# Batch 0 sorted in halves, with a Sinkhorn of its own, ahead of a fused attention and dense kernel

## The chip, the cores and the metric

One core of a Trainium2 chip, one launch. The metric is the device time of that launch in microseconds, the median of several runs. A profile of one further execution goes with it; its span runs from the first to the last instruction and is about one microsecond shorter than the time.

The engines: TensorE (PE, with its weight loads shown apart as PEld), VectorE (DVE), ScalarE (ACT), GpSimd (POOL) and SyncE (SP). Each runs its own list of instructions in order. DMA transfers are issued from SP's and POOL's lists and run on 16 shared DMA engines.

## The reference

Sinkhorn-sorted block attention on 4 batches of 8 heads, 768 tokens, 64 wide, followed by a dense layer pair:

```python
P = sort_net                                   # (4, 8, 8, 8), 8 blocks of 96 tokens
for _ in range(5):
    P = np.exp(P - P.max(-1, keepdims=True))
    P = P / (P.sum(-1, keepdims=True) + 1e-9)
    P = P / (P.sum(-2, keepdims=True) + 1e-9)
k_sorted = einsum('bhij,bhjcd->bhicd', P, k_blocks)      # v the same
attn = softmax(scale * q_block @ k_sorted_block.T)       # each block attends to its sorted block
x = (attn @ v_sorted_block) as (3072, 512)
h = x @ w_in                                   # 512 -> 2048
out = (s * relu(h)**2 + b) @ w_out             # 2048 -> 512
```

## The kernel before, in words

The 3072 tokens are eight tiles of 384 (TG): each batch gives two, `half` 0 (blocks 0 to 3) and `half` 1. `ffn1(t)` is the first dense layer of tile t: 8 steps `i`, each 8 matmuls of 128x384 (L361), a relu on ScalarE (L371) and a square on VectorE (L372). `ffn2(t)` is the second: 3 output tiles of 16 matmuls of 128x512 (L382), each ended by a sum with the bias on VectorE (L403) and a store. The order of all work is written out by hand: `manual_schedule` keeps each engine's list as the program issues it, and dictionaries of slots say which pieces of attention are put between the matmuls of the dense layers.

For a batch, `qk_piece` transposes q through a permuted identity and sorts k by the matrix `PD[b]`, 96 matmuls each, evicted in three pieces; `v_piece` sorts v (`permute` first puts v in the order that its matmuls want); `s_piece` forms scores for two heads of a half and takes exp on ScalarE; `p_piece` multiplies by v and divides by the row sums on VectorE (L303, L304); `t_piece` transposes the result on TensorE for batch 0, `t_dma` by DMA for the others.

The steady part runs from batch 1 on: `ffn1` of both tiles of batch b, then `ffn2` of both, in which the attention of batch b+1 is done (`halves`). Ahead of it stands the front:

- SP issues the load of `sort_net` and of v of batch 0 in four pieces (`v0f`); POOL issues q and k of batch 0 in three pieces each, builds the identity, and later w_in in eight pieces, w_out in four, and the next batches.
- The Sinkhorn of all four batches runs at once in 32 partitions: six or seven small VectorE operations (L184 to L194) and one exp (L177) for each of five steps. ScalarE copies one quarter of v between the steps (L156). TensorE warms up on zeros (L149).
- `build_pd(b)` spreads batch b's matrix to 128 partitions with a float matmul (L201) and five VectorE operations. Batch 0's stands in the front, the other three in `ffn1(1)`, where the bias is also summed (`make_bias`, L466 to L474).
- Then q, v and k of batch 0 are sorted whole, all of half 0's attention and the first two score pieces of half 1 follow, and `ffn1(0)` begins with three steps held open (`ahead=3`). The rest of half 1's attention stands in the slots of `ffn1(0)`.

PSUM is two pools: `psa` with three buffers of two banks, `psb` with two of one.

Of the kernel before, what the change touches and what calls it, by code (L numbers as in the profile page):

```python
# [22 lines left out]
def kernel(  # L23
# [47 lines left out]


    sn = const.tile([BH, NB, NB], FP)
    nc.sync.dma_start(out=sn, in_=sort_net.rearrange("b h i j -> (b h) i j"))
    v0f = gtp.tile([128, C2, D], FP, tag="gt", name="v0f")
    CV = C2 // 4
    for c in range(0, C2, CV):
        nc.sync.dma_start(out=v0f[:, c:c + CV, :].rearrange("p c d -> p (c d)"),  # L78
                          in_=raw[2][0][:, c * D:(c + CV) * D])

    RAW = {}

    def load(t, b, parts=1):
        ti = rawp.tile([128, C2, D], BF, tag=f"raw{t}", name=f"raw{t}")
        RAW[t, b] = ti
        n = C2 // parts
        for c in range(0, C2, n):
            nc.gpsimd.dma_start(out=ti[:, c:c + n, :].rearrange("p c d -> p (c d)"),
                                in_=raw["qkv".index(t)][b][:, c * D:(c + n) * D])

# [17 lines left out]
    nc.vector.memset(KS[0][:, :, :, C2:GAP], 0.0)  # L108
    eps = const.tile([BH, NB], FP)
    nc.vector.memset(eps, 1e-9)  # L110

    load("q", 0, 3)
    load("k", 0, 3)


    ident = const.tile([128, 128], BF)
    make_identity(nc, ident)
    idv = ident.rearrange("p (a e j z) -> p a e j z", a=NHP, e=2, j=NB)
    qid = const.tile([128, 2, 2, NHP, NB], BF)
    for e in range(2):  # L120
        nc.gpsimd.tensor_copy(out=qid[:, e], in_=idv[:, :, e].rearrange("p a j z -> p z a j"))
    emat = const.tile([BH, B, 128], FP)
    nc.gpsimd.memset(emat, 0.0)
    nc.gpsimd.affine_select(out=emat, in_=emat, pattern=[[-H, B], [-1, H], [0, 2 * NB]], base=0,
                            channel_multiplier=1, compare_op=ALU.not_equal, fill=1.0)
    wi = const.tile([128, NHP, d_ff], BF)
    wo = const.tile([128, NF, d_model], BF)

    def load_w():
        wiv = moe_w_in.rearrange("(a p) f -> p a f", p=128)  # L130
        for c in range(2):
            cs = slice(c * (d_ff // 2), (c + 1) * (d_ff // 2))
            for a in range(NHP):
                nc.gpsimd.dma_start(out=wi[:, a, cs], in_=wiv[:, a, cs])
        fill_vs(0)
        wov = moe_w_out.rearrange("(f p) n -> p f n", p=128)
        for c in range(4):
            fs = slice(c * (NF // 4), (c + 1) * (NF // 4))
            nc.gpsimd.dma_start(out=wo[:, fs, :], in_=wov[:, fs, :])
# [6 lines left out]
    def warm(n):  # L146
        for _ in range(n):
            z = psb.tile([128, 512], FP, tag="b", name="z")
            nc.tensor.matmul(out=z, lhsT=zeros[:, 0:128], rhs=zeros, start=True, stop=True)  # L149


    def permute(eng, b, src, cs=slice(0, C2), ds=slice(0, D)):
# [4 lines left out]
        else:  # L157
            eng.tensor_copy(out=o, in_=i)  # L158


    rstat = const.tile([BH, NB], FP)
    rrec = const.tile([BH, NB], FP)
    jsel = const.tile([128, NB], FP)
    bm = const.tile([128, 2 * 2 * NHP], FP)
    idle = [
        lambda: nc.vector.tensor_reduce(
            out=jsel, in_=ident.rearrange("p (h j z) -> p j h z", h=H, j=NB), axis=AX.XY, op=ALU.add),
        lambda: nc.vector.tensor_reduce(
            out=bm.rearrange("p (e z a) -> p e z a", e=2, z=2),
            in_=idv.rearrange("p a e j z -> p e z a j"), axis=AX.X, op=ALU.add),  # L170
    ]
    nc.vector.tensor_reduce(out=rstat, in_=sn, axis=AX.X, op=ALU.max)
    nc.vector.tensor_tensor(out=sn, in0=sn, in1=rstat.broadcast_to([BH, NB, NB]),
                            op=ALU.subtract)
    warm(30)
    for it in range(5):
        nc.scalar.activation(out=sn, in_=sn, func=AF.Exp)  # L177
        if it >= 1:
            permute(nc.scalar, 0, v0f, slice((it - 1) * CV, it * CV))
        if it == 2:  # L180
            load_w()
        if it in (1, 2):
            idle[it - 1]()
# [3 lines left out]
        if it == 4:  # L187
            break
# [8 lines left out]
    PD = {}  # L197

    def build_pd(b):
        pe = psb.tile([128, 512], FP, tag="b", name="pe")  # L200
        nc.tensor.matmul(out=pe[:, 0:NB * NB], lhsT=emat[:, b, :],  # L201
                         rhs=sn.rearrange("p i j -> p (i j)"), start=True, stop=True)
        tmp = rtp.tile([128, NB, NB], FP, tag="tmp", name="tmp")
        nc.vector.tensor_tensor(out=tmp, in0=pe[:, 0:NB * NB].rearrange("p (i j) -> p i j", j=NB),
# [10 lines left out]
            in0=spread(bm, [list(bm.ap[1]), [0, NB]]), scalar=rc,  # L215
# [3 lines left out]
    def evac(eng, out, in_):  # L219
        if eng == "A":  # L220
            nc.scalar.copy(out=out, in_=in_)  # L221
        else:
            nc.vector.tensor_copy(out=out, in_=in_)  # L223

    QT = {}

    def qk_piece(t, b, c0, eng, first=None):
        if t == "q" and c0 == 0:
            QT[b] = trp.tile([128, NG, 2, C2], BF, tag="qt", name="qt")
        src = RAW[t, b]  # L230
        mov = qid.rearrange("p e z a j -> p e z (a j)") if t == "q" else PD[b]
        dst = QT[b] if t == "q" else KS[b % 2]
        ps = psa.tile([128, CK, 2, NG], FP, tag="a", name="tp")
        for c in range(CK):
            for e in range(2):
                nc.tensor.matmul(out=ps[e * 64:(e + 1) * 64, c].rearrange("p z g -> p (z g)"),  # L236
                                 lhsT=src[:, c0 + c, :],
                                 rhs=mov[:, e].rearrange("p z g -> p (z g)"),
                                 start=True, stop=True)
        if first is not None:  # L240
            first()
        evac(eng, dst[:, :, :, c0:c0 + CK], ps.rearrange("p c z g -> p g z c"))
# [14 lines left out]
    def s_piece(b, half, hp):  # L257
        g0 = hp * NB + half * HB
        sc = psa.tile([128, 2, 512], FP, tag="a", name="sc")
        for n in range(HB):  # L260
            for e in range(2):
                pr = slice(e * 64, (e + 1) * 64)
                nc.tensor.matmul(out=sc[:, e, n * BLK:(n + 1) * BLK],  # L263
                                 lhsT=KS[b % 2][pr, g0 + n].rearrange("p z c -> p (z c)"),
                                 rhs=q_of(b, pr, hp, half * HB + n),
                                 start=True, stop=True)
        at = atp.tile([KR, 2, TG], BF, tag="at", name="at")
        nc.scalar.activation(out=at, in_=sc[0:KR, :, 0:TG], func=AF.Exp, scale=scale)  # L268
        AT[b, half, hp] = at

    def s_banks(b, half, hp):

        g0 = hp * NB + half * HB
        sc = [psb.tile([128, TG], FP, tag="b", name="scb") for _ in range(2)]
        for n in range(HB):
            for e in range(2):
                pr = slice(e * 64, (e + 1) * 64)
                nc.tensor.matmul(out=sc[e][:, n * BLK:(n + 1) * BLK],
                                 lhsT=KS[b % 2][pr, g0 + n].rearrange("p z c -> p (z c)"),
                                 rhs=q_of(b, pr, hp, half * HB + n),  # L280
                                 start=True, stop=True)
        at = atp.tile([KR, 2, TG], BF, tag="at", name="at")
        for e in range(2):
            nc.scalar.activation(out=at[:, e], in_=sc[e][0:KR], func=AF.Exp, scale=scale)
        AT[b, half, hp] = at
# [62 lines left out]
    def ffn1(t, slots, ahead=0):  # L348
# [16 lines left out]
        for i in range(ahead):  # L365
            part(i, (0, 1))
# [184 lines left out]
```

## Time and profile before

| | |
|---|---|
| median of 3 runs | 237.34 us (235.2 to 239.28) |
| the profiled execution, span | 236.1 us |
| TensorE, VectorE, ScalarE, GpSimd busy | 221.3, 122.9, 98.2, 55.4 us |
| first matmul of sorted v | 14.59 us |
| first dense layer of tile 0 begins | 31.84 us |
| second dense layer of tile 0 begins | 58.99 us |
| first dense layer of tile 2 begins | 91.08 us |
| each further batch | 50.0 us |

The times in the second part are starts in the profiled execution, from the timeline of TensorE's rows. The profile lists, for each engine, busy time and groups of like instructions by line; a waits view that says what ended the idle time before an instruction ("issue" where nothing in the profile did); a chain of the work that ended last; and busy time by stages, with the clock that TensorE was granted as a share of full speed.

### The profile page before, as it was taken

What the parts mean: (1) busy time and instruction counts of PE and PEld (TensorE: products, weight loads), DVE (VectorE), ACT (ScalarE), POOL (GpSimd) and SP (SyncE); (2) the same over time, 40 slices, a digit from 0 to 9 for tenths busy, and PEclk for the clock granted to TensorE, in tenths of its full rate; (3) what the DMA queues carried; (4) which work ended last, traced back from release to release, by engine and by line L of the source; (5) the groups of instructions that cost most, each with busy time, mean ns of one, the idle gap of its engine ahead of it and who ended that gap; (6) DMA issues with size and microseconds to landing.
All of it is one profiled execution on the core that took longest, in us unless ns stands there. A gap on an engine that the chain in (4) does not pass through costs nothing.

```text
span 236.1 us, 5888 instructions
## 1 busy us (share of the span) xinstructions
PE 221.3 (94%) x2584; PEld 130.8 (55%) x2607; DVE 122.9 (52%) x236; ACT 98.2 (42%) x123; POOL 55.4 (23%) x89
## 2 busy tenths in 40 slices
PE   7874898999998999999999999999999999999994
PEld 3553565655564655565555656656455656554453
DVE  6663426669755476444644764446355754342221
ACT  4783538554311524565212335665015255660000
POOL 7547500993663992000000000000000000000000
PEclk9998579999999999999999999999999999999999
DMA  6999999949999934920021187400112352001122
GB/s 144 286 210 193 206 209 218 190 74 205 137 190 203 170 67 124 147 37 0 3 89 50 44 114 160 86 3 3 44 47 88 64 119 45 0 1 47 52 81 90
DMA packets 37674, 25.03 MB, mean 106 GB/s; under 512 B 29200, under 2 KB 31504, under 8 KB 37648
## 3 DMA queue, kind: packets, MB, share of 16 engines
q0 software_dynamic: 17744, 12.85, 36.7%
q1 hardware_dynamic: 19904, 11.81, 20.3%
q8 instruction: 20, 0.33, 0.6%
q14 instruction: 6, 0.05, 0.1%
HBM read 27.27 MB, written 6.29 MB: 142 GB/s over the span
## 4 chain that ended last, share of the span: by engine, by line
PE 84%; DMA 4%; ACT 4%; issue 4%; DVE 2%; SPq 1%; DVEq 0%
PE hps L361 34%; PE ops L382 34%; DMA v0f<-in_v_dram 4%; PE tv L248 4%; PE tp L236 3%; PE pv L298 3%; PE sc L263 3%; PE ops L395 1%; ACT rt L371 1%; DVE x L304 1%; ACT qt L221 1%; PE z L149 1%; ACT vp L156 1%; PE tr L318 1%; SPq L78 1%
## 5 line engine op out<-in xcount | busy, mean ns | idle before, releaser
L361 PE MATMUL hps<-xt,wi 128*128 128x384 bf16 x512 | 86.3, 327 | 0.7 <-DVE x L304 0.5
L382 PE MATMUL ops<-wo,gt 128*128 128x512 bf16 x347 | 81.5, 379 | 2.2 <-issue 1.6
L371 ACT ACTIVATE rt<-hps 128x768 bf16<-128x768 f32 x64 | 51.7, 812 | 42.7 <-PE hps L361 41.1
L361 PEld LDWEIGHTS <-wi 128*128 128x128 bf16 x512 | 49.2, 98 | 32.9 <-issue 0.9
L372 DVE TENSOR_TENSOR gt<-rt 128x768 bf16<-128x768 bf16 x64 | 36.5, 572 | 44.4 <-ACT rt L371 44.2
L382 PEld LDWEIGHTS <-gt 128*128 128x128 bf16 x368 | 33.7, 98 | 37.0
L403 DVE SCALAR_TENSOR_TENSOR ot<-ops,s_bc,bias 128x512 f32<-128x512 f32 (+1 forms) x25 | 18.2, 729 | 37.2 <-PE ops L382 33.7
L268 ACT ACTIVATE at<-sc 112x768 bf16<-112x768 f32 x30 | 22.6, 809 | 32.7 <-PE sc L263 32.7
L158 POOL COPY vp<-rawv 128x384 bf16<-128x384 bf16 x24 | 20.3, 907 | 10.6 <-DMA rawv<-in_v_dram 10.6
L304 DVE TENSOR_TENSOR x<-pv,rec 96x512 bf16<-96x512 f32 x32 | 22.0, 687 | 1.1
L298 PEld LDWEIGHTS <-at 112*128 112x128 bf16 (+1 forms) x256 | 13.6, 106 | 7.2 <-ACT at L268 1.0
L223 DVE CAST vs<-tv 112x1024 bf16<-112x1024 f32 x11 | 13.3, 1223 | 6.6 <-PE tv L248 6.6
L99 POOL DMA_DIRECT2D qtok<-in_q_dram x16 | 12.4, 781 | 11.7 <-DMA rawv<-in_v_dram 6.7
L248 PE MATMUL tv<-pd,vp 128*64 128x64 bf16 x512 | 10.4, 197 | 5.0 <-issue 4.0
L221 ACT CAST vs<-tv 112x1024 bf16<-112x1024 f32 x5 | 5.1, 1021 | 22.9 <-PE tv L248 22.9
L298 PE MATMUL pv<-vs,at 112*128 112x66 bf16 (+1 forms) x256 | 14.6, 202 | 0.0
L248 PEld LDWEIGHTS <-vp 128*64 128x64 bf16 x512 | 9.2, 113 | 8.3 <-issue 7.3
L149 PE MATMUL z<-zeros 128*128 128x512 bf16 x37 | 11.9, 463 | 1.9 <-DVE zeros L103 1.2
L303 DVE RECIPROCAL rec<-pv 96x8 f32<-96x8 f32 x32 | 6.4, 200 | 13.9 <-PE pv L298 13.9
L263 PE MATMUL sc<-qt,ks 64*128 64x96 bf16 x240 | 9.0, 218 | 0.4 <-ACT vs L221 0.4
L223 DVE CAST ks<-tp 128x1024 bf16<-128x1024 f32 x7 | 8.3, 1218 | 0.2
L149 PEld LDWEIGHTS <-zeros 128*128 128x128 bf16 x39 | 4.0, 111 | 6.8 <-issue 2.8
(69 smaller groups left out, 107.9 us busy)
## 6 DMA issues: line engine op xcount, KB each, us to landing
out_dram<-ot SPq DMA_DIRECT2D x23, 256.0 KB, 2.0
rawv<-in_v_dram POOLq DMA_DIRECT2D x3, 768.0 KB, 11.9
rawk<-in_k_dram POOLq DMA_DIRECT2D x3, 768.0 KB, 7.9
wi<-in_moe_w_in_dram POOLq DMA_DIRECT2D x8, 256.0 KB, 11.8
wo<-in_moe_w_out_dram POOLq DMA_DIRECT2D x4, 512.0 KB, 14.2
v0f<-in_v_dram SPq DMA_DIRECT2D x4, 384.0 KB, 6.8
qtok<-in_q_dram POOLq DMA_DIRECT2D x16, 96.0 KB, 10.0
rawq<-in_q_dram POOLq DMA_DIRECT2D x3, 256.0 KB, 7.1
```

The source lines that it names most:

```text
L149: nc.tensor.matmul(out=z, lhsT=zeros[:, 0:128], rhs=zeros, start=True, stop=True)
L158: eng.tensor_copy(out=o, in_=i)
L223: nc.vector.tensor_copy(out=out, in_=in_)
L248: nc.tensor.matmul(out=ps[z * GAP:(z + 1) * GAP, d, :], lhsT=VP[b % 2][:, d0 + d, :], rhs=PD[b][:, :, z, :], start=True, stop=True)
L268: nc.scalar.activation(out=at, in_=sc[0:KR, :, 0:TG], func=AF.Exp, scale=scale)
L298: nc.tensor.matmul(out=pv[0:m, e, n * VW:(n + 1) * VW], lhsT=atf[:, c0:c0 + m], rhs=VS[b % 2][:, e * NG + g0 + n, :], start=True, stop=True)
L304: nc.vector.tensor_tensor(out=x[:, :, hp * 128:(hp + 1) * 128].rearrange("p n (e d) -> p e n d", e=2), in0=pvv[:, :, :, 0:D], in1=rec.unsq ...
L361: nc.tensor.matmul(out=H1[i][:, f, 0:TG], lhsT=wi[:, hp, fc:fc + 128], rhs=xt[:, :, hp, :], start=(hp == 0), stop=(hp == NHP - 1))
L371: nc.scalar.activation(out=rt, in_=h, func=AF.Relu)
L372: nc.vector.tensor_tensor(out=gt[:, 2 * i:2 * i + 2, :], in0=rt, in1=rt, op=ALU.mult)
L382: nc.tensor.matmul(out=ops, lhsT=gt[:, f, m * 128:(m + 1) * 128], rhs=wo[:, f, :], start=(f == 0), stop=(f == NF - 1))
L403: nc.vector.scalar_tensor_tensor(out=ot[:, ns], in0=ops, scalar=s_bc, in1=BIAS[0][:, ns], op0=ALU.mult, op1=ALU.add)
```

## The change

Batch 0's Sinkhorn becomes one of its own in 64 and 128 partitions, taking row sums by a float matmul against a mask (`rs`), with five VectorE and ScalarE operations for a step and v's quarters copied half by ScalarE, half by VectorE between the steps. The matrix comes out in two halves of columns (`pd0`). Only half 0 of k and v (blocks 0 to 3) is sorted ahead of `ffn1(0)`, by `kh` and `vh`, each with 32-column operands; half 1 stands in the slots of `ffn1(0)`. q of batches 0 and 1 is loaded in halves in another layout and transposed with the plain identity (`q_piece`, `q_half`). The other batches' Sinkhorn, still for all four together, runs inside `ffn1(1)` and `ffn2(0)` (`sink`), and their `build_pd` in `ffn2(0)` and `ffn2(1)`. w_in is loaded by columns, 512 at a time, and the identity is built ahead of POOL's loads. The first `part`s of `ffn1` are placed one by one in place of `ahead`.

```diff
+    s0 = const.tile([HI, NB], FP)
+    nc.sync.dma_start(out=s0, in_=sort_net[0].rearrange("h i j -> (h i) j"))
...
+    sn = const.tile([BH, NB, NB], FP)
+    nc.sync.dma_start(out=sn, in_=sort_net.rearrange("b h i j -> (b h) i j"))
+
+    ident = const.tile([128, 128], BF)
+    make_identity(nc, ident)
...
+    load_qh(0, 0, slice(0, 4))
     load("k", 0, 3)
+    load_qh(0, 0, slice(4, 8))
+    fill_vs(0)
+    load_wi(0, 512, slice(0, 2))
+    load_wi(0, 512, slice(2, 4))
+    load_wi(512, 1024)
+    load_qh(0, 1, slice(0, 8))
+    load_wi(1024, 1536)
+    load_wi(1536, 2048)
...
+    for it in range(4):
+        nc.scalar.activation(out=ex, in_=src, func=AF.Exp, scale=crec)
+        permute0(it)
...
+        nc.tensor.matmul(out=rs[:, 0, 0:NB], lhsT=msk.rearrange("p h g -> p (h g)"), rhs=ex,
+                         start=True, stop=True)
+        if it == 3:
+            q_piece(0, 0, 0, "A")
+            warm(2)
+        elif it == 2:
+            warm(3)
+        else:
+            warm(50, 16, 64)
+        nc.vector.reciprocal(out=rr, in_=rs[:, 0, 0:NB])
...
+        nc.vector.reciprocal(out=crec, in_=csum)
...
+    pd0(0)
...
+    kh(0, 0, "A", psa)
+    kh(0, 1, "D", psa)
+    pd0(1)
+    kh(0, 2, "A", psa)
+    vh(0, 0, "D", psb)
+    vh(0, 1, "A", psb)
+    vh(0, 2, "D", psa)
     s_piece(0, 0, 0)
+    vh(0, 3, "D", psa)
+    q_piece(0, 0, 2, "A")
     s_piece(0, 0, 1)
...
+    part(0, 0, (0,))
+    t_piece(0, 0, 1, "D")
     s_piece(0, 0, 3)
+    part(0, 0, (1,))
     p_piece(0, 0, 2)
+    kh(1, 0, "A", psb)
     p_piece(0, 0, 3)
+    part(0, 1, (0, 1))
...
+        if n == 1:
+            s0 = {0: [SK(3)], 1: [SK(4)], 2: [PDB(1)],
+                  4: [K(n, 0, "D"), K(n, 1, "A"), K(n, 2, "D")],
+                  7: [QF(n, 0, "D"), QF(n, 1, "A")],
+                  9: [V(n, 0, "D"), V(n, 1, "A"), V(n, 2, "D")]}
...
-    ffn1(0, {0: [SB(2)], 1: [P(0, 1, 0)], 2: [SB(3)], 3: [P(0, 1, 1)], 4: [P(0, 1, 2)],
-             5: [P(0, 1, 3)], 6: [TP(0, 1, 0, "A")], 7: [TP(0, 1, 2, "D")]}, ahead=3)
-    ffn1(1, {1: [PDB(1)], 3: [PDB(2)], 4: [make_bias], 6: [PDB(3)]}, ahead=3)
+    ffn1(0, {0: [KH(1, "D")], 1: [KH(2, "A"), QP(0, "D")],
+             2: [VH(0, "D"), VH(1, "A")], 3: [SC(0, 1, 0), VH(2, "D")],
+             4: [VH(3, "D"), SC(0, 1, 1)], 5: [P(0, 1, 0), QP(2, "D")],
+             6: [SC(0, 1, 2), P(0, 1, 1), TP(0, 1, 0, "A")],
+             7: [SC(0, 1, 3), P(0, 1, 2), TP(0, 1, 1, "D")]}, {0: 2, 1: 2})
+    part(1, 0, (0, 1))
+    p_piece(0, 1, 3)
+    t_piece(0, 1, 2, "A")
+    part(1, 1, (0, 1))
+    t_piece(0, 1, 3, "D")
+    ffn1(1, {2: [make_sel], 3: [SK(0)], 4: [make_bias], 5: [SK(1)], 7: [SK(2)]}, {0: 2, 1: 2})
     s0, s1 = halves(1, [(5, LD("k", 3)), (6, LD("v", 3)), (7, lambda: load_q_rows(3))])
+    s1[1] = [PDB(2)]
+    s1[2] = [PDB(3)]
```

`SK(it)` is `sink(it)`, one step of the loop that stood in the front before: on VectorE a row sum, reciprocal, product, column sum, reciprocal, product, with one exp on ScalarE ahead; step 0 has a maximum and a subtraction ahead of it and an added eps, step 4 ends after the first product.

## The prediction

> **What bounds the kernel now.** The page first: which engine fills the span, and whether its clock held.
>
> ```profile
> PE 221.3 (94%) x2584; PEld 130.8 (55%) x2607; DVE 122.9 (52%) x236; ACT 98.2 (42%) x123; POOL 55.4 (23%) x89
> PEclk9998579999999999999999999999999999999999
> q8 instruction: 20, 0.33, 0.6%
> ```
>
> TensorE fills 94%, so only its idle stretches and its slow stretch can be won. The clock row dips once, in the fourth to sixth slice (18 to 35 us). The third line is TensorE's own instructions: 20 packets for 5204 of them, 256 each. Next the chain in order of time, for the places where TensorE did not set the pace.
>
> ```profile
> 2.61 9.50 DMA v0f<-in_v_dram
> 12.13 1.50 ACT vp L156
> 13.63 1.83 ACT qt L221 x2
> ...
> 18.21 1.04 PE tv L248 x59
> 19.25 3.04 issue
> ...
> 32.05 2.77 PE hps L361 x16
> ...
> 59.42 0.59 PE ops L382 x2
> ...
> 91.24 20.80 PE hps L361 x128
> ```
>
> To 12.13 the chain is the load of v. At 19.25 TensorE stops for 3.04 us and waits for no engine. From 59 on (second dense layer) it is TensorE's rows nearly alone; from 91.24 the periods repeat, and no row of them is edited. So the change is worth what it does to two times: the start of the second dense layer (58.99) and its end (91.08). The stages around the stop, by the columns PE, PEld, DVE, ACT, POOL, clock, DMA share, GB/s:
>
> ```profile
> 18.82:22.23 3.41, 0.43 (x27) 0.35 (x22) 1.16 (x1) 0.44 (x1) 2.18 (x3) 0.96 1.09 183
> 22.23:25.64 3.41, 2.66 (x39) 1.67 (x40) 0.00 (x0) 2.98 (x4) 3.22 (x9) 0.50 1.12 204
> 25.64:29.05 3.41, 3.23 (x38) 2.33 (x40) 2.27 (x6) 0.87 (x3) 1.47 (x3) 0.50 1.23 206
> 29.05:32.47 3.42, 3.08 (x36) 2.27 (x35) 1.50 (x4) 2.24 (x3) 0.54 (x1) 0.54 1.25 207
> ```
>
> After the stop the clock is 0.50 for 10.2 us, and the DMA engines are full. Last the timeline, for the prices on VectorE:
>
> ```profile
> 7.42 0.21 DVE L184 TENSOR_REDUCE rstat<-sn 32x8 f32<-32x64 f32 x1
> ...
> 8.65 0.21 DVE L194 TENSOR_TENSOR sn<-sn,rrec 32x64 f32<-32x64 f32 x1
> 9.03 0.25 ACT L177 ACTIVATE sn<-sn 32x64 f32<-32x64 f32 x1
> ...
> 55.06 0.73 DVE L468 TENSOR_SCALAR bias<-cps,b_bc 32x512 f32<-32x512 f32 x1
> 55.83 2.31 DVE L471 SCALAR_TENSOR_TENSOR bias<-cps,b_bc,bias 32x512 f32<-32x512 f32 x3
> ```
>
> A Sinkhorn step is six VectorE rows from 7.42 to 8.86, 1.44 us, and an exp between, 0.45 with its hops; the bias sum holds VectorE 3.08.
>
> **The front, to the first dense layer.** Batch 0's own Sinkhorn with row sums on TensorE saves nothing by itself: its last step still copies v's last quarter, which lands at 12.12 now and, with the same loads sharing the engines, again. Without that cover the chain could end 1 to 2 us sooner. After 12.12 come the VectorE half of the copy (0.45: the 1024-element cast is 1.22, so 384 are about 0.45), reciprocal, product, reciprocal (0.2 each, 0.05 between) and the first half's matrix (0.28): 13.65. Before, the matrix was done at 14.09 and its first matmul, behind two qt evictions on ScalarE, ran at 14.59. So 0.9 won. The little warming matmuls (16 columns) lie between the row sums; bounds are the 64-column pair, 17 ns, and the 66-column pv, 32 ns, so 0.9 to 1.6 us for fifty, within a step of 1.9. I take them as free; at half clock they would be 3.2 and make the start up to 2 us later.
>
> Now the stop. It came before TensorE's row 698, a second (0.93, at 71.99) before row 1969. With float matmuls counted as the four records each leaves, these are 701 and 1981: 1280 apart, five blocks of 256. So TensorE waits for instructions, and the block edges lie at 189, 445, 701 and so on. Edge 445 was passed at 16.5, the block behind 701 usable at 22.29: 5.8 us later, with the DMA full. In the changed list five float matmuls stand ahead, so the edges are rows 430 (in the third half-k piece) and 686 (start of the fourth half-v piece). A piece is 32 pairs of 17 ns, 0.55. From 13.65, row 430 falls at 14.9 and row 686 is reached at 17.2; the block is there at 14.9 + 5.8 = 20.7. The stop stays, 3.5 us, and 1.6 is won against 22.29. Halved columns may make a pair cheaper than 17 ns (8.5 at the least), which would only lengthen this wait. The Trainium skill ("Runtime: NRT & Kernel Launch", Instruction fetch mechanics) has the same blocks but says the fetch is mostly hidden; by it the wait would fall out, here it measured 3.04.
>
> From 20.7 the half-tile pieces run as a relay. Rest of v 0.55, q transposes 0.4 (12 by the 0.043 of tr at most 0.5), ScalarE's qt copy 0.8 and exp 0.81, pv, then VectorE's reciprocal and product 0.95, transposes and copies 0.5, twice over since scores 2 and 3 come late, and the half-1 k piece 0.55: the rest of the first dense layer starts at 29.2 with eight of its matmuls done (31.84 before, with none).
>
> **Inside the first dense layers.** First tile: 56 matmuls by 0.1625 (20.8 for 128) are 9.1. Put in: two k and four v pieces 3.3, 24 transposes 0.8, four scores 1.0, three pv 0.8, eight tr 0.35. Together 15.4, and about 1.6 of waits for buffers that VectorE empties late: 46.2. The split doubles k's and v's instructions, and this half stands on TensorE's path. Then the tile's end: relu 0.81, square 0.55, reciprocal and product 0.95, copy 0.3 until the next tile's second quarter, and again pv, 0.95, tr, 0.3: 51.3, of which 2.6 is work. Second tile: 9.0 and the bias matmuls 1.0. The second dense layer starts at 61.2, against 58.99: **2.2 lost**, although three pe matmuls have left this stage.
>
> **The new wait.** The other batches' Sinkhorn now stands on VectorE between the squares, and PDB(1), after 12 matmuls of the second layer, waits for its last product. VectorE's rows from 55.4 on, in program order: selectors 0.6; five squares with gaps 2.9; step 0 (max, subtract, exp, seven rows) 2.5; bias 3.1; steps 1 and 2, 1.46 each; step 3 with its exp 1.8; step 4 with its exp 1.1; 0.5 of waits for a relu and an exp. 15.4: done at 70.8. Nothing hides this: but for those waits VectorE is never idle in it, and the first output tile's sum and store stand behind it too. TensorE stands at PDB(1) at 61.2 + 2.6 = 63.8, and behind it are all of the second layer, k, q and v of batch 1. **6.9 lost.** Each PDB is 0.36 on TensorE and moves behind the 58.99 mark: **1.1**. q of batch 1 by 48 transposes instead of 96 matmuls (1.64): between 0.8 at 17 ns and 2.1 at 0.043; I take 1.5, **0.1 won**.
>
> After 6.9 idle the clock will drop, since 3.04 was enough. Coming back cost 10.2 us of half clock in sparse work (5.1 lost) and, at the start, 4.0 in dense warm matmuls (2.0 lost: rows 0.43 apart until 4.98, later 0.21). The second layer is dense, so near the lower: **2.3**. The Trainium skill ("TensorE: Matmul & The Clock Gate", Part 1) gives one window of 3.4 us for the return, 1.7 by it; the 10.2 here is three.
>
> Put at nothing: w_in by columns, q in halves, constants and wo are the same bytes at 205 GB/s; w_in's first columns land near 17 and are used at 24.7, its last near 27 (used 41), wo near 38 (used 56), sn near 13 (used 56.7). The selector pattern now goes ahead of POOL's first load, 0.6; k's last third then lands near 13 and is used at 14.7. Without these covers each would cost its own lateness. q's runs are shorter (384 bytes; qtok's 128-byte loads took 10 us), with ten or more to spare.
>
> **Sum.** 2.2 + 6.9 + 1.1 - 0.1 + 2.3 = 12.4. The profiled execution spans 236.1; the median is 237.34, 1.2 more, which I keep: 236.1 + 12.4 + 1.2 = **249.7 us**.
>
> **Rivals.** (1) The wait at PDB(1) is short: for it, VectorE is only 52% busy over the span, and before it was just 1.4 late at 60.41 though it had three PDBs and the bias in this stage. Without the wait and its clock loss, 249.7 - 6.9 - 2.3 = **240.5**, not slower by 2%. It decides once the wait is below 1.6. Against: 15.4 of rows with no gap. (2) The fetched block comes in time: 249.7 - 3.5 = **246.2**. For it, instruction packets after 30 us started within 2 us of their edge; against, the DMA is as full as it was then. (3) The 3.5 stop drops the clock in the front too, as 3.04 did: the relay's TensorE rows are 5 us, doubled, with some 2 hidden in its waits, plus 3: **252.7**. Against: the stop may straddle two of the clock's windows.
>
> **How the numbers follow.** Forecast 0.47, (3) 0.25, (2) 0.15, (1) 0.10, something that makes it really faster 0.03. (2) without the 2.3 of clock and with the six inner pieces at half price (1.7 less) is 242.2; (3) with the 5.1 return is 255.5. Low 242, high 255.5; the forecast's own range is 247 to 251.5. This measurement tells about 2% from no change: 232.6 and 242.1. Faster 0.03, within 0.10, slower 0.87.
>
> **What would show it.** Right: a wait of TensorE near 7 us just after the second layer starts, released by VectorE's last sn row; VectorE without idle time ahead of it; an issue gap of 3 us at a half-v piece; the clock row dipping near 65 to 75; periods from the third tile on unchanged at 50.0. Wrong: second layer starting before 59, or PDB(1) unwaited.

## The result and the profile after

The changed kernel takes 257.13 us (median of four, 254.47 to 258.12) against 238.06 (four, 235.2 to 239.28): a ratio of 1.083, 95% interval 1.072 to 1.094. It is slower, as forecast, but by more: 249.7 had been predicted and 255.5 was the upper end. The profiled execution is the fastest of the four (254.47, span 252.3), 16.2 us longer than before's span.

The page: the share of TensorE first, its clock, its instruction packets.

```profile
PE 232.4 (92%) x2810; PEld 141.6 (56%) x2832; DVE 128.7 (51%) x273; ACT 97.1 (38%) x131; POOL 57.8 (23%) x86
PEclk9999999999976999999999999999999999999999
q8 instruction: 22, 0.36, 0.6%
```

There is one dip, at 70 to 80 us, and none in the front. That is a trap: the trace has no clock record before 28.6 us, and the row then shows full speed. The rows themselves tell the clock. The chain in order of time:

```profile
6.78 2.77 PE z L129 x50
...
10.07 2.77 PE z L129 x50
...
17.30 2.67 PE kh L309 x48
19.97 2.56 PE vh L323 x48
...
23.14 1.84 issue
...
107.15 20.80 PE hps L490 x128
```

The chain of the front is no longer the load of v. It is the two blocks of fifty small warming matmuls (128x64 by 16 columns), 57 ns each, then the half pieces, then the stop. From 107 us the periods are 50.0 us as before. From TensorE's timeline, the points that the prediction dated (in square brackets the idle time ahead of a row and what ended it):

```profile
17.23 2.74 PE L309 MATMUL kh<-pdh,rawk 128*64 128x32 bf16 x96
...
24.97 0.99 PE L323 MATMUL vh<-pdh,vp 128*64 128x32 bf16 x30 [1.84 <-issue]
...
34.44 0.86 PE L490 MATMUL hps<-xt,wi 128*128 128x384 bf16 x4 [0.24 <-ACT xt L236]
...
67.39 2.54 PE L514 MATMUL ops<-wo,gt 128*128 128x512 bf16 x11
75.50 0.66 PE L353 MATMUL pe<-sn,emat 32*128 32x64 f32 x2 [5.57 <-DVE sn L340]
```

Three half-k pieces take 2.74, 0.91 each; in the first dense layer one takes 0.68. So the front ran at half clock. The second dense layer starts at 67.39 instead of 58.99 (8.4 lost) and its pair ends 39.6 later instead of 32.1 (7.5 lost); together 15.9 of the 16.2. Who waited, and the stretch around the new wait (columns as in the prediction):

```profile
PE pe L353 <- DVE sn L340: 5.6, 1, 5.6
...
DVE rr L286 <- PE rs L277: 4.7, 3, 2.2
```

```profile
65.00:70.00 5.00, 4.87 (x26) 2.35 (x24) 4.72 (x11) 2.40 (x4) 1.47 (x2) 1.00 0.73 49
70.00:75.00 5.00, 0.00 (x0) 0.00 (x0) 3.94 (x18) 0.77 (x3) 1.67 (x2) 0.80 0.00 0
75.00:80.00 5.00, 4.50 (x28) 1.92 (x30) 2.19 (x8) 0.00 (x0) 0.00 (x0) 0.51 0.06 22
```

VectorE is busy 4.7 of 5 us ahead of the wait, TensorE does nothing for 5.6, and then runs at half clock to 79.9. That half of the prediction came as told. The second line of the waits is the one that had not been priced: VectorE stands 4.7 us for row sums, and 4.0 of them behind the two blocks of small matmuls:

```profile
10.11 0.21 DVE L286 RECIPROCAL rr<-rs 128x8 f32<-128x8 f32 x1 [2.21 <-PE rs L277]
...
13.40 0.21 DVE L286 RECIPROCAL rr<-rs 128x8 f32<-128x8 f32 x1 [1.79 <-PE rs L277]
```

### The profile page after: what moved, and what is told of

Same layout as the page of the kernel before. It is cut to its first block, busy times and chain, and to the rows that moved or that the text cites. A ratio compares the mean times of both kernels' runs of the same rounds, so it can differ in the third digit from the quotient of the medians.

```text
span 252.3 us, 6386 instructions
## 1 busy us (share of the span) xinstructions
PE 232.4 (92%) x2810; PEld 141.6 (56%) x2832; DVE 128.7 (51%) x273; ACT 97.1 (38%) x131; POOL 57.8 (23%) x86
## 4 chain that ended last, share of the span: by engine, by line
PE 84%; DVE 8%; ACT 3%; issue 3%; DMA 1%; DVEq 0%; ACTq 0%
PE ops L514 31%; PE hps L490 30%; PE pv L442 3%; PE sc L420 3%; PE z L129 3%; PE tv L398 3%; PE vh L323 2%; PE tp L388 2%; DVE gt L503 2%; PE ops L527 1%; PE kh L309 1%; ACT rt L502 1%; DVE x L448 1%; DVE bias L612 1%; PE rs L277 1%
## 5 line engine op out<-in xcount | busy, mean ns | idle before, releaser
L514 PE MATMUL ops<-wo,gt 128*128 128x512 bf16 x347 | 83.4, 385 | 2.2 <-issue 1.6
L503 DVE TENSOR_TENSOR gt<-rt 128x768 bf16<-128x768 bf16 x64 | 35.9, 561 | 47.4 <-ACT rt L502 47.2
L428 ACT ACTIVATE at<-sc 112x768 bf16<-112x768 f32 x16 | 12.1, 806 | 21.0 <-PE sc L420 21.0
L424 ACT ACTIVATE at<-sc 112x768 bf16<-112x768 f32 x16 | 12.5, 808 | 12.3 <-PE sc L420 12.3
L116 POOL DMA_DIRECT2D qtok<-in_q_dram x16 | 12.3, 778 | 10.2 <-DMA rawv<-in_v_dram 5.2
L238 DVE CAST vs<-tv 112x1024 bf16<-112x1024 f32 x9 | 10.7, 1221 | 5.9 <-PE tv L398 5.9
L129 PE MATMUL z<-zeros 128*64 128x16 bf16 (+1 forms) x127 | 12.4, 238 | 1.4 <-DVE zeros L120 1.2
L129 PEld LDWEIGHTS <-zeros 128*64 128x64 bf16 (+1 forms) x128 | 7.9, 155 | 3.5 <-issue 2.1
L236 ACT CAST vs<-tv 112x1024 bf16<-112x1024 f32 x3 | 3.1, 1018 | 16.8 <-PE tv L398 16.8
L323 PE MATMUL vh<-pdh,vp 128*64 128x32 bf16 x256 | 6.7, 199 | 1.8 <-issue 1.8
L238 DVE CAST ks<-tp 128x1024 bf16<-128x1024 f32 x6 | 7.1, 1220 | 1.8 <-PE tp L388 1.6
```

The costliest lines, as they stand in the source:

```text
L129: nc.tensor.matmul(out=z[0:m, 0:w], lhsT=zeros[:, 0:m], rhs=zeros[:, 0:w], start=True, stop=True)
L424: nc.scalar.activation(out=at.rearrange("p e (t c) -> p e t c", c=CQ), in_=sc[0:KR, :, 0:TG].rearrange("p e (c t) -> p e t c", c=CQ), func ...
L503: nc.vector.tensor_tensor(out=gt[:, 2 * i:2 * i + 2, :], in0=rt, in1=rt, op=ALU.mult)
L514: nc.tensor.matmul(out=ops, lhsT=gt[:, f, m * 128:(m + 1) * 128], rhs=wo[:, f, :], start=(f == 0), stop=(f == NF - 1))
```

## The experiments

Three theories were set against each other. A: the small warming matmuls delay the row sums and leave the clock low. B: VectorE's late Sinkhorn makes TensorE wait at the pe matmul. C: TensorE's front is paced by the fetch of its own instructions. The rival to A was that the halved pieces and the order of loads cost the front.

**Wide warming in place of small.**

```diff
-    warm(16, 16, 64)
+    warm(2)
...
-            warm(50, 16, 64)
+            warm(6)
```

> The changed kernel with its small warming matmuls (64x16) replaced by 512-column ones of the same half-clock time: 16 small by 2 wide, each fifty by 6 wide. Theory A (the front ran at half clock to 29 us because small matmuls do not bring the clock up, and their 57 ns each delay the row sums): half-k pieces fall from 0.91 to 0.55 us each, the second dense layer of tile 0 starts near 61 instead of 67.4, span 245 to 247 against 252.3. 102 fewer TensorE rows also move the instruction-block edge out of the short pieces, so the 1.84 us stop should be gone, which is counted in this. Rival (the halved k and v pieces and the order of the loads cost the front): pieces at full clock perhaps, but the second layer still starts at 65 or later, span 250 or more. The wait at the pe matmul of batch 1 stays near 5.6 under both.

Measured: 254.62 us, 1.071 of before (1.066 to 1.076), span 251.8.

```profile
6.71 2.72 PE L129 MATMUL z<-zeros 128*128 128x512 bf16 x6
9.48 1.46 PE L129 MATMUL z<-zeros 128*128 128x512 bf16 x6
...
14.17 1.69 PE L309 MATMUL kh<-pdh,rawk 128*64 128x32 bf16 x96 [0.43 <-DVE pdh L260]
...
21.10 0.61 PE L323 MATMUL vh<-pdh,vp 128*64 128x32 bf16 x15 [3.97 <-issue]
...
65.34 2.54 PE L514 MATMUL ops<-wo,gt 128*128 128x512 bf16 x11
```

The same six matmuls take 2.72 and then 1.46: the clock came up at 9.5. A half-k piece is 0.56, and the first one starts 3.1 us earlier. So far theory A holds. But TensorE then stands 3.97 us for instructions instead of 1.84, the clock falls (the next half-v piece takes 1.04), and only 2 us are left at the second layer. The expectation that the stop would go was wrong by its own arithmetic: a matmul with its weight load is two instructions, so 102 fewer move the edge by 204 of a block of 256, that is 26 matmuls earlier. The stop came 15 matmuls before the end of half-v piece 2 instead of 2 into piece 3, with 8 score matmuls between: 25. By its numbers (65.34 and 251.8) the rival came true in this run; the run that issues the weights later, below, tells the two apart.

**No small matmuls at all.**

```diff
-    warm(16, 16, 64)
...
-        else:
-            warm(50, 16, 64)
```

> The changed kernel with the small warming matmuls left out and nothing in their place. It tells their two costs apart. Theory A, delay: the four row sums come at VectorE's own pace, first half-k matmul near 14.5 instead of 17.2. Theory A, clock: TensorE is idle between the row sums, so it stays at half clock (a half-k piece still 0.9 us, matmuls of 512 columns 0.43 apart) to about 29 us; second dense layer of tile 0 starts near 63, span about 248. Rival (the small matmuls did hold something up, and the clock falls lower or later without them): second layer later than 67.4, span above 252.

Measured: 254.02, 1.069 (1.064 to 1.075), span 250.8.

```profile
13.76 2.74 PE L306 MATMUL kh<-pdh,rawk 128*64 128x32 bf16 x96
...
20.55 0.19 PE L320 MATMUL vh<-pdh,vp 128*64 128x32 bf16 x1 [1.49 <-issue]
...
32.89 1.22 PE L487 MATMUL hps<-xt,wi 128*128 128x384 bf16 x4 [0.24 <-ACT xt L236]
...
66.00 2.54 PE L511 MATMUL ops<-wo,gt 128*128 128x512 bf16 x11
```

Without them the first half-k matmul comes at 13.76, where the prediction had put it (13.65), against 17.23. That is the whole delay. The second layer, though, starts only 1.4 earlier than in the changed kernel (63 had been expected). Now compare this kernel with the wide warming at the stop: one ran the pieces at half clock, the other at full. By the prediction's count a stop lies one block, 128 matmuls, behind the edge at which the block is asked for. Counted from that edge (15.4 here, 14.9 there), the block came after 5.1 and 6.2 us. Half clock did not lengthen the fetch; it only let TensorE reach the stop later. The clock counts behind the stop, where this kernel, at half clock until 33.8, took 12.3 us to the rest of the first layer, and the other, at half clock until 26.5, took 10.6.

**The pe matmul later.**

```diff
-            s0 = {0: [SK(3)], 1: [SK(4)], 2: [PDB(1)],
-                  4: [K(n, 0, "D"), K(n, 1, "A"), K(n, 2, "D")],
-                  7: [QF(n, 0, "D"), QF(n, 1, "A")],
-                  9: [V(n, 0, "D"), V(n, 1, "A"), V(n, 2, "D")]}
+            s0 = {0: [SK(3)], 1: [SK(4)],
+                  4: [QF(n, 0, "D"), QF(n, 1, "A")], 6: [PDB(1)],
+                  8: [K(n, 0, "D"), K(n, 1, "A"), K(n, 2, "D")],
+                  10: [V(n, 0, "D"), V(n, 1, "A"), V(n, 2, "D")]}
```

> The changed kernel with the pe matmul of batch 1 moved from slot 2 to slot 6 of the second dense layer of tile 0, its q transposes ahead of it in slot 4, k to slot 8 and v to slot 10. The front is unchanged. Theory B (TensorE stands 5.6 us for VectorE's last Sinkhorn row and then runs 6.8 us at half clock): the wait falls to 0 to 1 us, no slow stretch follows, span 252.3 - 5.6 - 2.3 + 0.5 = 245. Rival (VectorE is the bound of this stage, so the wait only moves to the k copies, the output sums or the scores of batch 1): span 249 or more, with a new wait of 3 us or more behind slot 6.

Measured: 249.76, 1.049 (1.042 to 1.057), span 248.0.

```profile
32.44 1.04 PE L309 MATMUL kh<-pdh,rawk 128*64 128x32 bf16 x32
...
69.34 4.26 PE L514 MATMUL ops<-wo,gt 128*128 128x512 bf16 x19
...
77.45 0.40 PE L353 MATMUL pe<-sn,emat 32*128 32x64 f32 x2 [0.55 <-DVE sn L340]
```

The wait is 0.55, no slow stretch follows (pe 0.40), and the pair takes 33.4 instead of 39.6: 6.2 won, B holds. The front is the same code as in the changed kernel, and yet the second layer starts 2 us later: the half-k piece at 32.44 still takes 1.04, the clock came up at about 38 us here and at 29 in the profiled execution of the changed kernel. So one and the same front varies by 2 us between two executions.

**The kernel before with small warming.**

```diff
-    warm(30)
+    warm(5)
+    warm(105, 16, 64)
```

> The kernel before, with its 30 warming matmuls of 512 columns at the start replaced by 5 of them and 105 small ones (64x16), so that TensorE still issues without a gap to about 9 us. Theory A (small matmuls do not bring the clock up): the 64 q matmuls that took 1.20 us take about 2.4, the k and v pieces double too, the clock comes up late, first dense layer starts 2 to 4 us later than 31.8, span 238 to 240. Rival (any matmul without a gap brings it up): 1.20 as before, span 236 to 237.

Measured: 237.15, 0.999 of before (0.995 to 1.003), span 233.3.

```profile
9.04 1.92 PE L238 MATMUL tp<-qid,rawq 128*64 128x64 bf16 x62
...
20.61 0.71 PE L238 MATMUL tp<-pd,rawk 128*64 128x64 bf16 x21 [2.49 <-issue]
...
30.73 2.77 PE L363 MATMUL hps<-xt,wi 128*128 128x384 bf16 x16
```

The same q matmuls in the kernel before:

```profile
9.61 1.20 PE L236 MATMUL tp<-qid,rawq 128*64 128x64 bf16 x64
```

The clock part of A is right: 62 matmuls take 1.92, where 64 took 1.20, though TensorE had issued without a gap since 1.2. (The first clock record is at 17.3 us, behind the wider q and v pieces.) Its price is not: the first dense layer starts at 30.73, 1.1 earlier than in the kernel before. Half clock ahead of the stop is hidden by the wait for instructions. What counts is the stretch behind the stop, and there this kernel was at full clock from 24.2 us where the kernel before was not until 32.2.

**Theory C by itself: weights issued later.** In the changed kernel with wide warming, POOL holds back most of the weights until half-v piece 2 has been copied (`gsc` is one element, s and b go with them):

```diff
     vh(0, 2, "D", psa)
+    nc.gpsimd.tensor_copy(out=gsc, in_=VS[0][0:1, 0, 0:1])
+    for f0 in (512, 1024, 1536):
+        load_wi(f0, f0 + 512)
...
+        nc.gpsimd.dma_start(out=wo[:, fs, :], in_=wov[:, fs, :])
```

> The changed kernel with the wide warming matmuls, and in addition the loads of w_in from column 512 on, of the two scalars and of w_out are issued by POOL only after half-v piece 2 has been copied, so that the DMA engines are nearly idle when TensorE's next block of instructions is fetched. Theory C (the front is bound by the instruction fetch: one block of 128 matmuls each 5 to 6 us while the loads fill the DMA engines; the stop was 3.97 us with wide warming alone): the stop falls to 1.5 us or less, the clock then stays up, second dense layer of tile 0 starts at 61 to 62 against 65.3, span 247 to 248. Rival (the fetch takes its 6 us whatever the load): stop 4 us, 65.3 and 251.8 as without the later loads; or the later weights come too late for the first layer and TensorE waits for wi.

Measured: 255.4, 1.066 (1.059 to 1.074), span 250.6: stop 3.48, second layer at 64.23. A miss for the test more than for the theory: the loads issued ahead kept the DMA share at 1.25 from 14 to 16 us, when the block was asked for. The same with the edit of the late pe matmul:

> Wide warming, later loads and the late pe matmul together: all three suspected costs of the changed kernel taken away at once. If they add: second layer at 61 to 62, no wait at the pe matmul, span 248.0 - 69.3 + 61.5 = 240, a time near 242. What then is left over the kernel before (some 2 to 4 us) is the halved k and v pieces and the pe matmuls inside the dense layers. Rival (VectorE is late whatever the slot once the front is faster, since its Sinkhorn then starts no earlier): wait at pe of 2 to 4 us and a span of 243 to 246.

Measured: 247.5, 1.041 (1.036 to 1.046), span 245.6, where 242 and 240 had been expected: stop 3.23, second layer at 65.79, wait at pe 0.57. The kernel before got the same cure, behind its second k piece:

```diff
-            load_w()
+            fill_vs(0)
...
     qk_piece("k", 0, CK, "D")
+    nc.gpsimd.tensor_copy(out=gsc, in_=KS[0][0:1, 0, 0, 0:1])
+    load_w()
```

> The kernel before with only the loads of the two weight matrices issued later: POOL issues them after the second k piece has been copied. Theory C: the 3.04 us stop of TensorE falls below 1, the clock does not dip, the first dense layer starts near 28 instead of 31.8, span 232 to 233.5, time near 234. Rival (the fetch takes its 6 us whatever the load): stop of 3 us as before and a span of 236, or more if the weights come late.

Measured: 237.74, 0.999 (0.996 to 1.002), span 236.0. DMA share and GB/s are the last two columns:

```profile
14.00:16.00 2.00, 1.46 (x81) 1.43 (x83) 1.03 (x2) 2.00 (x3) 0.00 (x0) 1.00 0.36 70
16.00:18.00 2.00, 1.30 (x83) 1.21 (x79) 1.34 (x2) 0.76 (x2) 0.00 (x0) 1.00 0.00 0
```

```profile
17.05 1.27 PE L235 MATMUL tp<-pd,rawk 128*64 128x64 bf16 x69 [0.70 <-issue]
...
20.50 0.26 PE L247 MATMUL tv<-pd,vp 128*64 128x64 bf16 x5 [0.77 <-issue]
...
27.77 2.77 PE L360 MATMUL hps<-xt,wi 128*128 128x384 bf16 x16
...
54.44 1.03 PE L381 MATMUL ops<-wo,gt 128*128 128x512 bf16 x3
58.65 2.77 PE L235 MATMUL tp<-pd,rawk 128*64 128x64 bf16 x96 [3.18 <-DVE bias L473]
```

With the DMA engines empty the block that TensorE asked for at 17.05 was usable at 20.50, 3.45 us, where it took 5.8 under full load. The DMA records of the instruction queue (q8) show where the difference lies. In the kernel before, the packet with this block started at 19.93, 3.5 us after the edge, and TensorE went on 2.36 later; here it started at 18.15, 1.1 after the edge, and TensorE went on 2.35 later. The block does not take longer; it waits longer to start while the loads fill the engines. The stop of 3.04 is now two, of 0.70 and 0.77 (between them 69 and 59 matmuls, one block), the clock stays up, the first layer starts 4.1 us earlier and the second 4.6. C holds. And then all of it is given back (third tile at 91.03 instead of 91.08): the scalar b, behind the weights in POOL's list, now lands at 55.5, TensorE waits 3.18 for the bias sum, runs 3.4 us at half clock and waits 0.88 for an output sum.

The changed kernel with POOL's copy one piece earlier, so that the engines are empty in time (share 0.04 from 14 to 16 us), with wide warming and the late pe matmul:

```diff
     kh(0, 2, "A", psa)
+    nc.gpsimd.tensor_copy(out=gsc, in_=KS[0][0:1, 0, 0, 0:1])
+    load_wi(0, 512, slice(0, 2))
+    load_wi(0, 512, slice(2, 4))
+    load_qh(0, 1, slice(0, 8))
+    for f0 in (512, 1024, 1536):
+        load_wi(f0, f0 + 512)
...
```

> The changed kernel with wide warming, the late pe matmul, and all of w_in, the second half of q and w_out issued only after half-k piece 2 has been copied, so that the DMA engines are empty from about 12 us, before TensorE passes the block edge at 14. Theory C: fetch 3.5 us as in the kernel before with later loads, stop 1.5 us or less instead of 3.2, the clock does not fall, rest of the first layer at 28 instead of 30.4, second layer near 62.5, span near 242. Rival (the weights are then late for the first layer, or the later blocks are fetched under full load and stop TensorE there instead): second layer at 65 or later and a span of 245 or more.

```profile
13.22 1.70 PE L312 MATMUL kh<-pdh,rawk 128*64 128x32 bf16 x96 [0.61 <-DVE pdh L263]
...
17.14 0.42 PE L326 MATMUL vh<-pdh,vp 128*64 128x32 bf16 x15 [0.96 <-issue]
...
27.31 0.86 PE L493 MATMUL hps<-xt,wi 128*128 128x384 bf16 x4 [0.23 <-ACT xt L239]
...
59.86 4.48 PE L517 MATMUL ops<-wo,gt 128*128 128x512 bf16 x20
```

The stretch in which the block is asked for, with wide warming alone (first line) and here (second; the last two columns are DMA share and GB/s):

```profile
14.00:16.00 2.00, 1.83 (x116) 1.83 (x117) 0.72 (x2) 0.73 (x3) 1.85 (x4) 1.00 1.24 203
...
14.00:16.00 2.00, 2.00 (x137) 2.00 (x132) 1.42 (x3) 1.14 (x3) 1.41 (x3) 1.00 0.04 8
```

Measured: 243.41, 1.020 (1.015 to 1.026), span 239.4. From the first half-k matmul to the end of the stop it is 3.9 us instead of 6.9, and the second layer starts at 59.86: 7.5 earlier than in the changed kernel and 0.9 later than before. (The clock did fall, against the expectation: 0.50 from 17.7 to 21.1.) So most of the front's 8.4 us were the small matmuls, the fetch and the clock. But the kernel before gains by later weights too, and against it (54.44) this one is still 5.4 later. Up to the first layer the two are level (27.31 and 27.77); the two first layers take 32.6 here and 26.7 there. That is the price of sorting half 1 inside them, and it stays.

**VectorE's share in the wait.** In the changed kernel the bias sum went behind the pe matmul of batch 1.

```diff
-    ffn1(1, {2: [make_sel], 3: [SK(0)], 4: [make_bias], 5: [SK(1)], 7: [SK(2)]}, {0: 2, 1: 2})
+    ffn1(1, {2: [make_sel], 3: [SK(0)], 5: [SK(1)], 7: [SK(2)]}, {0: 2, 1: 2})
...
-            s0 = {0: [SK(3)], 1: [SK(4)], 2: [PDB(1)],
+            s0 = {0: [SK(3)], 1: [SK(4)], 2: [PDB(1), make_bias],
```

> The changed kernel with the bias sum (16 cps matmuls, 3.08 us of VectorE) moved from slot 4 of the first layer of tile 1 to just after the pe matmul of batch 1. Theory B (the wait at that matmul is the sum of VectorE's rows, back to back): the wait falls from 5.6 to about 2.5, the clock perhaps stays up, part comes back as waits for the first output sum; span 247 to 250. Rival (the Sinkhorn chain is paced by the hops to ScalarE and the relus, the bias sum lies in its gaps): wait still above 4.5, span above 251.

Measured: 253.01 (two runs, 250.03 and 255.98, the second profiled, too few for a verdict): the wait was 3.54, so 2.0 shorter. The span, 254.2, missed the 247 to 250: in this execution the clock came up only at 40 us, and the second layer started at 69.43. From one and the same square (the last ahead of Sinkhorn step 0, at 61.93 in the changed kernel, 65.28 here) to the end of VectorE's last product it is 13.4 us and here 10.3: the whole 3.1 of the bias rows came off, as B has it. The wait shrank by less because the 16 cps matmuls (1.05) had moved too, so that TensorE reached the pe matmul sooner; the expectation had left that out.

**w_in by columns alone, in the kernel before.**

```diff
-            for a in range(NHP):
-                nc.gpsimd.dma_start(out=wi[:, a, cs], in_=wiv[:, a, cs])
...
+        for f0 in range(512, d_ff, 512):
+            nc.gpsimd.dma_start(out=wi[:, :, f0:f0 + 512], in_=wiv[:, :, f0:f0 + 512])
```

> The kernel before with one part of the change alone: w_in loaded by columns, 512 at a time for all four row groups (the first 512 in two loads), in place of eight loads of 1024 columns each. The prediction put it at nothing, since the same bytes land long before they are used: span 235.5 to 236.7, time equal. Rival (shorter rows make the loads slower, or the smaller number of issues on POOL lets them start sooner): first dense layer moved by more than 0.5 us from 31.8.

Measured: 237.91, 1.001 (0.998 to 1.005); first dense layer at 32.13 (31.84 before). Nothing, as predicted for this part.

**Can the front's gain be kept?** The kernel before with later weights was followed to where it lost its 4.6 us. First the two scalars were loaded in the front:

```diff
+    for t, src in ((s_bc, moe_s), (b_bc, moe_b)):
+        nc.gpsimd.dma_start(out=t, in_=src.to_broadcast([128, 1]))
     warm(30)
```

> The kernel before with the weights issued after the second k piece, as in the run before it, and the two scalars s and b loaded in the front instead of behind w_out. The earlier run reached the second dense layer at 54.4 instead of 59.0 but stood 3.2 us there, since b landed at 55.5 and the bias sum with it. Theory C: with b early that wait goes, second layer at 54.4, span 236.1 - 4.5 = 231.6, time near 233, faster by about 2%. Rival (VectorE or the late w_out hold this stage in another way, so the 4.5 us are given back once more): span 235 to 236.

Measured: 239.03, 1.006 (1.003 to 1.010). Second layer at 53.45, then

```profile
69.39 1.82 PE L385 MATMUL ops<-wo,gt 128*128 128x512 bf16 x4 [4.44 <-DVE ot L406]
```

```profile
65.84 0.77 POOL L99 DMA_DIRECT2D qtok<-in_q_dram  x1 [2.93 <-DMA rawv<-in_v_dram]
66.66 1.90 POOL L476 COPY bias<-bias 32x512 f32<-32x512 f32 x3
```

POOL stood for batch 2's earlier loads before it could issue more of them, and the bias copies stood behind in its list. With those loads (`loads2`) moved behind the copies:

```diff
-    ffn1(1, {1: [PDB(1)], 3: [PDB(2)], 4: [make_bias], 6: [PDB(3)]}, ahead=3)
+    ffn1(1, {1: [PDB(1)], 3: [PDB(2)], 4: [make_bias, loads2], 6: [PDB(3)]}, ahead=3)
```

> The kernel before with the weights issued late and the two scalars early, as in the run before, and in addition batch 2's loads issued by POOL behind its three copies of the bias row instead of ahead of them. [...] Theory (the 5.5 us won in the front were given back only by POOL's order): that wait goes, the pair of second layers takes its 32.1 us, third tile from 85.6 instead of 91.1, span 231, time near 233, faster by 2 to 2.5%. Rival (another engine's lateness takes the wait's place, such as v's sort for batch 1 or batch 2's loads being late later on): span 234 or more.

Measured: 238.14, 1.003 (1.000 to 1.006). The pair now ended at 85.5, but

```profile
89.37 22.95 PE L364 MATMUL hps<-xt,wi 128*128 128x384 bf16 x123 [3.90 <-DMA xt<-x]
```

the DMA transposes of the third tile's input lay among batch 3's loads. Those loads were written one stage later in the program, here and in the last version of the changed kernel:

```diff
-    s0, s1 = halves(1, [(5, LD("k", 3)), (6, LD("v", 3)), (7, lambda: load_q_rows(3))])
+    s0, s1 = halves(1)
...
-        ffn1(2 * b, {})
+        ffn1(2 * b, {3: [LD("k", 3), LD("v", 3), lambda: load_q_rows(3)]} if b == 1 else {})
```

> The kernel before with the weights issued late, the scalars early, batch 2's loads behind the bias copies, and batch 3's loads moved from the second dense layer of tile 0 to the first layer of tile 2, so that the DMA transposes of tile 2's input are not among loads of 2.4 MB. The run before stood 3.9 us at the third tile for such a transpose (landed in 9.4 us, 4.2 in the kernel before) and then ran 6.8 us at half clock. Theory: third tile from 85.5, span 231, time 232 to 233.5, faster by 2%. Rival (the 5 us are given back a fourth time, at batch 2's or 3's first use): span 235 or more.

> The changed kernel with wide warming, the late weights, the late pe matmul, and batch 3's loads moved to the first layer of tile 2. Its run without the last edit had a trace of 239.4 and a median of 243.4, with 0.4 us of wait for a transpose at the third tile. If such transposes are what makes its other runs longer: median 241 or less. If not: 243 again.

Measured: 240.7, 1.011 (1.007 to 1.015), with a wait of 6.04 at the third tile; and 244.88, 1.031 (1.027 to 1.035), with 0.40 at the third tile as without the edit. The edit did not do what was meant: POOL has no reason to wait at a place in the program. In the kernel before it moved the issue of batch 3's k from 70.24 to 76.70, still ahead of the transposes at 80.07 and 86.97, and the wait grew from 3.90 to 6.04. (In the second, the clock came up at 12.4 instead of 4.1 and the front was 1.9 later, out of 3.5 in the span.) So POOL was made to wait:

```diff
+    def gate3():
+        nc.gpsimd.tensor_copy(out=gsc, in_=GT[2][0:1, 7, 0:1])
...
-        ffn1(2 * b, {3: [LD("k", 3), LD("v", 3), lambda: load_q_rows(3)]} if b == 1 else {})
+        ffn1(2 * b, {3: [gate3, LD("k", 3), LD("v", 3), lambda: load_q_rows(3)]} if b == 1 else {})
```

> As the run before, but POOL really holds batch 3's loads back: a one-element copy of tile 2's first-layer output goes ahead of them on POOL, which waits for it. In the run before POOL had issued them at 76.7 us as early as ever, and the transposes of tile 2's input (80.1 and 87.0) lay among them; the third tile waited 6.0 us. Theory: no such wait, third tile from 85.5 instead of 91.1, clock 1.0 throughout, span 231 to 232, time 232.5 to 234, faster by about 2%. Rival (the transpose is slow for another reason, such as batch 2's loads or the output stores): wait of 3 us or more again, span 236 or more.

```profile
54.19 1.03 PE L385 MATMUL ops<-wo,gt 128*128 128x512 bf16 x4
...
86.61 20.97 PE L364 MATMUL hps<-xt,wi 128*128 128x384 bf16 x128
```

Measured: 234.71 (232.12 to 236.65), 0.985 of before, 0.979 to 0.991; span 232.9. The third tile starts at 86.61 instead of 91.08 with no wait; 1.4 us come back in the next period (51.4 instead of 50.0, a wait of 1.24 for an output sum at 117). By the interval this kernel is 1 to 2% faster than the kernel before, a little less than the 2% expected. It is the kernel before with four edits to when loads are issued, and nothing of the change.

## Why the prediction was right and wrong

**The sign and the second half were right.** The wait at the pe matmul: 6.9 told, 5.6 measured, released by VectorE's last product, with VectorE busy ahead of it. The clock behind it: 2.3 told; half clock from 75.5 to 79.9 is 2.2. The pe matmuls inside the layers 0.36 each and the transposes of q 1.46 (1.5 told). Of the 10.2 in the pair 7.5 came: the wait was 1.3 shorter, and the kernel before's second stop (0.93) has gone. The late pe matmul gave 6.2 of it back. Loads at nothing: the run by columns agrees, and in the trace after TensorE waits for no load.

**The step that failed** is the front, told at 2.2 lost and measured at 8.4, and in it one sentence: that the little warming matmuls are free. They had been priced by 17 to 32 ns from rows of full clock; they took 57. The bound at half clock was also named (3.2 us for fifty, "up to 2 us later"), and put aside. Measured was 2.84 for fifty, and it was paid twice, as VectorE's waits of 2.21 and 1.79 for a row sum behind each fifty; the first half-k matmul came 3.6 later than told. Taken out alone, the small matmuls give back only 1.4 (nothing in their place) or 2.1 us (wide ones) at the second layer; the rest goes to the longer stop (3.97 with wide ones) and to the half clock behind it (until 33.8 us with none). Nothing in the trace of before says that small matmuls raise the clock, and the dense warming that did so there had been removed by the change: this could have been read from the diff. The Trainium skill ("TensorE: Matmul & The Clock Gate", Part 1) has the clock released after a busy window of about 3.4 us. Here TensorE issued small and half-width matmuls almost without a gap from 6 to 23 us and the clock stayed at half to 29; six matmuls of 512 columns in the first of the same places brought it up by 9.5.

The other 2.6 of the 6.2 are three smaller terms. From the first half-k matmul to the end of the stop 7.7 (7.05 told). From there to the rest of the first layer 9.5 (8.5 told; 9.5 from the same matmul in the run with all loads late too, with the clock up for two thirds of it): the relay between ScalarE, VectorE and TensorE was undersized. The two first layers 32.95 (32.0 told). The stop itself came exactly at the instruction that had been worked out, the third matmul of the fourth half-v piece. The fetch took 5.7 us from the edge (5.8 told). The stop was 1.84 and not 3.5 because TensorE, at half clock, needed 3.9 us from the edge to it instead of 2.3.

**What the sum does not hold.** In the profiled execution the misses make 3.5 (6.2 more in the front, 2.7 less in the pair), and its time lies 2.2 above its span instead of 1.2. The median lies 2.7 above that execution. The likely reason is the clock coming up later: the two other traces with the same front (late pe matmul, moved bias sum) have it up at 38 and 40 us instead of 29 and start the second layer 2 us later. No trace of the slower executions of the changed kernel itself shows it.

**The rivals.** A short wait did not come. A block in time did not come either; even with empty DMA engines it came 0.8 to 1.0 late. The point made for it, packets within 2 us of their edge after 30 us, does not hold everywhere: the packet ahead of the second stop before started at 70.58, 4.2 us after its edge at 66.4. The clock lost in the front too (252.7) came nearest in its number, but not by its mechanism: the clock did not fall at the stop, it had not been up.

## What to carry to other kernels

Price filler at the state it will meet, not at the state of the rows it is priced from, and ask what stands behind it in its engine's list: matmuls that only keep an engine busy are on the path of whatever waits for the next useful one. A stretch of many short instructions is bounded by their fetch; when a stop shows no releaser, look at what the DMA engines carry at that moment, and move bulk loads away from it. A gain in the front is kept only if everything the moved loads feed is followed to its first use: here it was lost three times, to a scalar, to a list's order and to a transpose among loads.

## What the runs showed of the hardware

- TensorE takes its instructions in blocks of 256, two for a matmul with its weight load. Taking 102 and 116 matmuls out of the front moved the stop 25 and about 11 matmuls earlier (26 and 12 by the arithmetic).
- From passing one edge to the use of the next block it took 5.8 us with the DMA engines full (before) and 3.45 with them empty (before with later weights). The packet started 3.5 and 1.1 us after the edge; from its start to the next matmul it was 2.4 us in both. The same 177 half-piece matmuls and the stop took 6.9 us and 3.9. The Trainium skill ("Runtime: NRT & Kernel Launch", Instruction fetch mechanics) calls the crossing mostly hidden; where the matmuls of a block take less than these times, it was not, even with empty engines (0.77 and 0.96).
- Small matmuls (64x16, 57 ns apart) did not raise the clock: with five wide ones at their head TensorE issued for 7.9 us without a gap, and the q matmuls behind them ran at half speed (before with small warming). For one front the moment it rose differed between executions: 29, 38 and 40 us.
- A DMA transpose among batch loads made the layer behind it wait 3.9 and 6.0 us, and with the loads held back not at all.
